# One group of small products a unit in batches 1 to 3 of a linear-attention and mixer kernel

## The chip, the cores and the metric

The kernel runs on one core of one Trainium2 chip. The metric is the device time of one execution in microseconds (us); a lower time is better. A difference of under about 0.3% (1.4 us here) can't be told from no change with this kernel.

Engines carry the names that the profile gives them: PE is the matrix engine (PEld its weight loads), DVE the vector engine, ACT the scalar engine, POOL the third elementwise engine, SP the engine that issues the transfers. Products are written to PSUM, from which ACT or DVE copy them to SBUF.

## The reference

Two blocks stand one behind the other. The first is a gated linear attention over 4 batches, 8 heads, 768 steps and 48 channels; the second a mixer on the 4 x 768 x 384 result.

```
f = sigmoid(f_logit)
for t in range(S):
    state = f[:, :, t, :, None] * state + einsum('bhd,bhe->bhde', k[:, :, t], v[:, :, t])
    y[:, :, t] = einsum('bhd,bhde->bhe', q[:, :, t], state)
x = y laid out as (batch, seq, heads * head_dim)
h = x^T @ U @ V                       # low rank, over the sequence
u = x + h^T
out = u + relu(u @ w_ch1) @ w_ch2
```

The einsum of the state is the outer product of a step's key with its value. Everything is in float32.

## The kernel before

**Units.** A unit is one pair of heads of one batch: 4 batches of 4 units, 16 in all, numbered `n` from 0. The sequence of a unit is cut into 12 chunks of 64 steps. Gates are turned into running products inside a chunk, so that queries and keys can be scaled by them (DVE, functions `gates`, `keep`, `keys`, `read` and `queries` of `prepare`). What is left for PE is five groups of small products for each unit (function `attend`):

- `kept` (L1002, tile `pt`): 12 transposes of the scaled keys; ACT copies the result to `kb` (L1006), and `spread` makes `whole` (L1012), the chunks' decays, on ACT.
- `states` (L1026, tile `ds`): 24 products of `kb` with v, each chunk's addition to the state; ACT copies `ds` to `added` (L1034).
- `scan` (L1051): DVE runs through `added` with the decays in `whole`; the states go to `st` by POOL (batches 1 and 2) or ACT (batch 3).
- `scores` (L975, tile `sc`): 24 products of keys and queries inside the chunks; DVE masks them into `A` (L988).
- `read` (L1069, tile `y`): 22 products of queries with the states `st`, followed on ACT by a copy of two columns, `seen` (L1076).
- `inner` (L1087, added onto `y`): 24 products of `A` with v; ACT copies `y` to `x` (L1093).

Each of these products is run as two passes (the trace shows 48 records for 24 products). They use parts of the array, 48 or 64 rows by 64 columns; the transposes use 64 rows by 128 columns.

**What fills PE between them.** While the attention of batch b runs, the mixer of batch b-1 supplies large products over the whole array: `pz` (L300), `po` (L355, batch 0's) and `pw` (L389, the other batches). `Fill` spreads them by cost over the pieces that `steps` yields: each piece, an empty one too, is preceded by its share of large products. `joined` puts several functions into one piece and yields empty pieces in place of the others, so that the shares stay.

**The order in a step.** Step n of `steps` issues one piece with `inner` of n-2, `scores` of n-1 and `kept` of n; later one with `read` of n-1, `states` and `scan` of n. Between them lie the fronts of unit n+1 (`gates`, `keep`, `keys`, and `read_back`, `queries`, the place of which depends on `behind`). So each unit has two groups of small products, with large products around each.

**PSUM.** Tiles with the tag `big` (two banks each) have three buffers: `pt`, `ds`, `sc` and `y` take them in turn, in the order in which they are allocated; the mixer's `pp`, `put` and `pu` use the same ones. `pz`, `po` and `pw` have two buffers of their own. `kb` and `whole` have a single buffer.

**Who orders what.** PE runs in the order of the code everywhere. DVE and ACT run in the order of the code up to the beginning of batch 2; behind that a scheduler orders them, with raised priority for the mask and the scan. SP is ordered by the scheduler from the end of batch 0. In batch 3 DVE also forms sums of the weights (`sum_of_w`, L929) at the pieces listed in `turns`.

Of the kernel before, what the change touches and what calls it, by code (L numbers as in the profile page):

```python
# [10 lines left out]
F32 = mybir.dt.float32  # L11
# [10 lines left out]
PAD = 64  # L22
# [542 lines left out]
def factored_path(ctx, tc, q, k, v, f_logit, moe_U, moe_V, moe_w_ch1, moe_w_ch2, out, ok):  # L565
# [5 lines left out]
    B, H, S, D = q.shape  # L571
    P = nc.NUM_PARTITIONS
# [4 lines left out]
    HP = H // 2  # L577
# [5 lines left out]
    NU = B * HP  # L583
# [17 lines left out]
    ps_big = ctx.enter_context(tc.tile_pool(name="ps_big", bufs=3, space=bass.MemoryType.PSUM))  # L601
# [23 lines left out]
    def packed(n, nm):  # L625

        i = 2 * n + (nm == "q")
        return w2.rearrange("p c d -> p (c d)")[:, i * 2 * NBL * D : (i + 1) * 2 * NBL * D]

    def load(n, *names):  # L630

        b, hp = divmod(n, HP)
        for nm in names:
            if nm == "v":
                v_tiles[n] = three.tile([P, NBL, 2, D], F32, name="v_nat")
            for par in range(2):
                head = src[nm][b, 2 * hp + par]
                if nm in "kq" and n < HP:
                    if par == 0:
                        nc.sync.dma_start(  # L640
                            out=packed(n, nm).rearrange("p (h t) -> p h t", h=2),
                            in_=src[nm][b, 2 * hp : 2 * hp + 2].rearrange("h (p c) d -> p h (c d)", p=P),
                        )
                    continue
                if nm == "v" and par:

                    for s in range(2):
                        nc.sync.dma_start(
                            out=v_tiles[n][(1 - s) * C : (2 - s) * C, :, par, :],
                            in_=head.rearrange("(c s p) d -> s p c d", s=2, p=C)[s],  # L650
                        )
                    continue
                if nm == "v" or n < TURNED:
                    dst = v_tiles[n] if nm == "v" else nat[n % 2][nm]
                    nc.sync.dma_start(out=dst[:, :, par, 0:D], in_=head.rearrange("(c p) d -> p c d", p=P))
                    continue
                head = head.rearrange("(c i) d -> i c d", i=NB)
                for part in range(2):
                    p0 = par * PAD + part * NB
                    n_ch = min(NB, D - part * NB)  # L660
                    nc.sync.dma_start(  # L661
                        out=raw[n % 2][nm][p0 : p0 + NB, :].rearrange("p (c d) -> p c d", d=NB)[:, :, 0:n_ch],
                        in_=head[:, :, part * NB : part * NB + n_ch],
                    )
# [248 lines left out]
    w_places, x_places, v_places, room = [], [], [], {}  # L913
# [43 lines left out]
    def attend(n):  # L957

        b, hp = divmod(n, HP)
        T = units[n]  # L960
        vt = v_tiles[n]
        rows = [slice(par * PAD, par * PAD + D) for par in range(2)]
        chunk = [slice(c * C, (c + 1) * C) for c in range(NCH)]

        part = [slice(s * C, (s + 1) * C) for s in range(2)]
# [48 lines left out]
        def halves_of(n):  # L1014
            return [slice(0, D // 2), slice(D // 2, D)] if n == HP - 1 else [slice(0, D)]

        def states():

            M = D if b else PAD
            ds = ps_big.tile([P, 2, 512], F32, name="ds", tag="big")  # L1020
            for c in range(NBL):
                for s in range(2):
                    for par in range(2):

                        i = (c + (s & par)) % NBL
                        nc.tensor.matmul(  # L1026
                            ds[par * PAD : par * PAD + M, s, c * D : (c + 1) * D],
                            lhsT=T["kb"][part[s ^ par], par, i, 0:M], rhs=vt[part[s ^ par], c, par, :],
                            start=True, stop=True,
                        )  # L1030

            for r in rows if b else [slice(0, P)]:
                for e in halves_of(n):
                    nc.scalar.copy(  # L1034
                        added[r, 1:].rearrange("p (e c s) -> p e c s", c=NBL, s=2)[:, e],
                        ds[r, :, 0 : NBL * D].rearrange("p s (c e) -> p e c s", e=D)[:, e],
                    )
# [40 lines left out]
        def inner():  # L1078
# [17 lines left out]
            )  # L1096
            del units[n], v_tiles[n]

        return [kept, states, scan, scores, read, inner, mask, spread]

    ahead, here = {}, {}

    def front(n, *names):

        if n >= NU:
            return []
        if n not in ahead:
            names_of = ("gates", "keep", "keys", "read_back", "queries", "gates_end", "unpack_k", "unpack_q")
            ahead[n] = dict(zip(names_of, prepare(n)))
        return [ahead[n].pop(nm) for nm in names if nm in ahead[n]]  # L1110

    def rear(n, *names):

        if not 0 <= n < NU:
            return []
        if n not in here:
            here[n] = dict(zip(("kept", "states", "scan", "scores", "read", "inner", "mask", "spread"), attend(n)))
        return [here[n].pop(nm) for nm in names if nm in here[n]]

    def joined(*groups):  # L1120

        groups = [g for g in groups if g]
        for _ in groups[1:]:
            yield lambda: None
        if groups:
            yield lambda: [f() for g in groups for f in g]

    def steps(first, last):

        def behind(n):  # L1130

            return HP + 3 <= n < NU - 1

        for n in range(first, last):
            if n < NU:
                yield from joined(rear(n - 2, "inner"), rear(n - 1, "scores"), rear(n, "kept"))
            else:
                for piece in rear(n - 2, "inner") + rear(n - 1, "scores"):
                    yield lambda: None
                    yield piece  # L1140
            if behind(n):
                yield from front(n, "read_back", "queries")
            if n + 1 < NU and n + 1 not in v_tiles:
                load(n + 1, "v")
            yield from front(n + 1, "gates", "keep", "keys")
            yield from joined(rear(n - 1, "read"), rear(n, "states", "scan"))
            if not behind(n + 1):
                yield from front(n + 1, "read_back", "queries")
            if n + 1 == last:
                yield from rear(n - 1, "inner")  # L1150
                if n + 2 < NU:
                    load(n + 2, "v")

    def attention(pieces, fill):

        for piece in pieces:
            fill()
            piece()
        fill.rest()

    def beside(pieces, calls):

        for i, piece in enumerate(pieces):
            yield piece
            while calls and calls[0][0] <= i:
                calls.pop(0)[1]()
        assert not calls
# [15 lines left out]
    with tc.manual_schedule(engines={nc.vector.engine, nc.scalar.engine}):  # L1183
# [111 lines left out]
        n = len(m.seconds) // (NBL // 2)  # L1295
        todo, after = m.seconds[:-n], m.seconds[-n:]

        attention(second, Fill(todo, 10 + 10 * HP - (len(start) + len(m.firsts) - 1 - EARLY)))
        n = 2 * HP + 2
# [3 lines left out]
        pieces, fill = steps(n - 1, 3 * HP + 1), Fill(m.main, 10 * HP - 3)  # L1303
# [3 lines left out]
    for b in range(2, B - 1):  # L1307
        if b > 2:
            pieces, fill = steps(b * HP + 1, (b + 1) * HP + 1), Fill(m.main, 10 * HP)
# [1 line left out]
        attention(pieces, fill)  # L1311
        m = start_mixer(b, after)

    turns = 5, 7, 8, 13, 14, 15, 16, 18, 19, 22, 27
    early_sums = len(W_SUMS) - len(turns)
    for i in range(early_sums):
        sum_of_w(i)
    pieces = beside(steps((B - 1) * HP + 1, NU + 1),
                    [(t, lambda i=i: sum_of_w(i)) for i, t in enumerate(turns, early_sums)])
    todo = m.first(0) + m.ready(0) + m.halved(0)  # L1320
    attention(pieces, Fill(todo[:-1], 33))

    mixers = [m, mixer(B - 1)]
    NP = NBL // 2
# [10 lines left out]
    todo = of(0, "sums_of_x") + of(0, "fewer")  # L1335
    todo[5:5] = of(1, "sums_of_x") + m.second(0)[-1:]
    for i in range(len(pairs)):
        ahead, behind = of(i + 1, "fewer"), of(i, "second")
# [356 lines left out]
```

## Time and profile before

| | |
|---|---|
| Median of 3 runs | 466.35 us (465.92 to 467.19) |
| Span of the profiled execution | 463.2 us, first to last instruction |
| Median less span | 3.15 us (the page gives no time of the profiled execution beside its span) |
| PE busy | 455.2 us, 98% of the span |
| DVE, ACT, POOL busy | 351.4, 170.4, 48.5 us |
| Granted PE clock | 0.999 |

Batch 0's attention fills the first 35 us or so, batches 1 to 3 run from there to 316 us beside the large products of the batch before, and from 316 us on only the mixer of batches 2 and 3 is left. A row of the timeline gives the start of a run of like instructions, how long it took from its start to its modelled end, and in brackets the idle time before it with its releaser. Since products are pipelined, a run's end lies behind the next one's start; what a run takes of PE is the distance from its start to the next one's start.

### The profile page before, as it was taken

To read this page: it belongs to the slowest core of one execution; us is meant where nothing else is said; L and a number is where in the kernel's file an instruction comes from. 1 tells how busy PE (TensorE), PEld (TensorE's weight loads), DVE (VectorE), ACT (ScalarE), POOL (GpSimd) and SP (SyncE) were. 2 spreads that over 40 slices of the span, in tenths; PEclk is the share of its full clock that TensorE was granted. 3 is DMA by queue.
4 is the path that set the end of the run, shared out by engine and by line. 5 is a ranking of instruction groups with operands and counts; after the bars stand their busy time and mean duration, and the time that the engine had idled before them with its cause. 6 is when DMAs were issued, how large, how long until landed. Compare 5 with 4: busy or idle time off the path is not lost.

```text
span 463.2 us, 13016 instructions
## 1 busy us (share of the span) xinstructions
PE 455.2 (98%) x5639; PEld 394.5 (85%) x5639; DVE 351.4 (76%) x585; ACT 170.4 (37%) x323; POOL 48.5 (10%) x56
## 2 busy tenths in 40 slices
PE   8999999999999999999999999999999999999997
PEld 5886888875666578999898888899989999999996
DVE  6778788979999677676765559977797887858652
ACT  6785776562333143323322323451412311212200
POOL 2002445634112001010000000000000000000000
PEclk9999999999999999999999999999999999999999
DMA  9959997577777604504633030100000000000001
GB/s 194 186 139 212 227 217 180 150 119 103 124 113 118 107 18 53 78 1 89 77 52 74 14 61 4 28 3 21 18 1 1 35 1 23 13 1 35 1 36 39
DMA packets 148583, 34.35 MB, mean 74 GB/s; under 512 B 136934, under 2 KB 146982, under 8 KB 148518
## 3 DMA queue, kind: packets, MB, share of 16 engines
q1 hardware_dynamic: 147718, 33.29, 37.1%
q8 instruction: 46, 0.75, 0.7%
q10 hardware_dynamic: 800, 0.15, 0.2%
q14 instruction: 19, 0.16, 0.1%
HBM read 28.70 MB, written 4.72 MB: 72 GB/s over the span
## 4 chain that ended last, share of the span: by engine, by line
PE 80%; DVE 11%; ACT 3%; DMA 2%; issue 2%; SPq 2%; DVEq 0%; ACTq 0%
PE pw L389 27%; PE pz L300 21%; PE pp L495 12%; PE po L355 5%; PE y L1069 2%; PE sc L975 2%; PE ds L1026 2%; PE y L1087 2%; PE pt L1002 1%; SPq L661 1%; DVE late L894 1%; PE pt L777 1%; DVE late L876 1%; PE pt L835 1%; DMA other<-in_f_logit_dram 1%
## 5 line engine op out<-in xcount | busy, mean ns | idle before, releaser
L300 PE MATMUL pz<-uT,w 128*128 128x256 f32 x492 | 111.5, 382 | 0.3
L300 PEld LDWEIGHTS pz<-uT,w 128*128 128x128 f32 x492 | 91.7, 190 | 12.9 <-ACT uT L289 0.6
L389 PE MATMUL pw<-zw,w_raw 128*128 128x192 f32 x216 | 38.0, 329 | 0.0
L389 PE MATMUL pw<-w,z_all 128*128 128x192 f32 x216 | 37.3, 327 | 0.0
L335 ACT ACTIVATE z_all<-pz 128x512 f32<-128x512 f32 x33 | 19.6, 598 | 45.1 <-PE pz L300 44.7
L389 PEld LDWEIGHTS pw<-w,z_all 128*128 128x128 f32 x216 | 35.3, 190 | 0.5
L389 PEld LDWEIGHTS pw<-zw,w_raw 128*128 128x128 f32 x216 | 35.1, 190 | 0.6 <-issue 0.3
L101 POOL TENSOR_TENSOR w<-w_y,w_r 128x384 int32<-128x384 int32 x24 | 31.5, 1311 | 37.0 <-DVE w_y L100 22.5
L876 DVE TENSOR_TENSOR_SCAN late<-fz,late 128x768 f32<-128x768 f32 x12 | 21.1, 1755 | 9.4 <-ACT fz L871 9.3
L488 ACT ACTIVATE other<-other 128x512 f32<-128x512 f32 x18 | 11.3, 630 | 40.3 <-DVE other L204 40.3
L355 PE MATMUL po<-w,zw 128*128 128x384 f32 x72 | 25.2, 495 | 0.0
L355 PE MATMUL po<-w,z_all 128*128 128x384 f32 x72 | 24.7, 493 | 0.0
L1057 POOL COPY st<-added 128x576 f32<-128x576 f32 x8 | 12.4, 1556 | 113.8 <-DVE added L1051 113.8
L988 DVE TENSOR_TENSOR A<-sc,causal 128x768 f32<-128x768 f32 x16 | 15.2, 953 | 8.5 <-PE sc L975 8.5
L355 PEld LDWEIGHTS po<-w,zw 128*128 128x128 f32 x72 | 13.2, 190 | 9.6 <-issue 0.8
L894 DVE TENSOR_TENSOR_SCAN late<-fz,other 128x768 f32<-128x768 f32 x12 | 21.0, 1750 | 0.2
L355 PEld LDWEIGHTS po<-w,z_all 128*128 128x128 f32 x72 | 13.3, 190 | 8.9 <-DVE o L204 0.6
L488 ACT ACTIVATE z_all<-z_all 128x512 f32<-128x512 f32 x12 | 7.6, 631 | 34.1 <-DVE z_all L204 34.1
L1034 ACT COPY added<-ds 48x576 f32<-48x576 f32 (+2 forms) x29 | 17.8, 619 | 4.5 <-PE ds L1026 4.1
L495 PE MATMUL pp<-v_nat,late 128*128 128x128 f32 x152 | 19.1, 275 | 0.0
L1069 PEld LDWEIGHTS y<-st,qT 48*64 48x64 f32 x704 | 13.6, 137 | 6.2 <-issue 4.5
L98 DVE TENSOR_SCALAR w_y<-w_y 128x384 f32<-128x384 f32 (+3 forms) x27 | 12.1, 449 | 8.8 <-ACT w_y L91 8.8
(233 smaller groups left out, 872.1 us busy)
## 6 DMA issues: line engine op xcount, KB each, us to landing
w_raw<-in_moe_w_ch_dram SPq DMA_DIRECT2D x18, 384.0 KB, 3.6
out_dram<-o SPq DMA_DIRECT2D x17, 192.0 KB, 1.9
v_nat<-in_v_dram SPq DMA_DIRECT2D x16, 144.0 KB, 3.8
v_nat<-in_v_dram SPq DMA_DIRECT2D x32, 72.0 KB, 3.5
zw<-in_moe_w_ch_dram SPq DMA_DIRECT2D x6, 384.0 KB, 5.1
out_dram<-o SPq DMA_DIRECT2D x14, 96.0 KB, 2.2
w<-in_k_dram SPq DMA_DIRECT2D x4, 288.0 KB, 4.1
w<-in_q_dram SPq DMA_DIRECT2D x4, 288.0 KB, 4.2
```

Source lines behind the costliest of these rows:

```text
L101: nc.gpsimd.tensor_tensor(dst.bitcast(I32), shaped(y.bitcast(I32)), shaped(r), ALU.add)
L300: nc.tensor.matmul(pm[:, i * 2 * P : (i + 1) * 2 * P], lhsT=w1[:, m, o : o + P], rhs=uT[a][:, m, :], start=(m == 0), stop=(m == NDC - 1))
L335: nc.scalar.activation(z[a, c][:, k : k + 2, :].rearrange("p i t -> p (i t)"), pm, AF.Relu)
L355: nc.tensor.matmul(pm, lhsT=z[a, i // NI][:, i % NI, s * P : (s + 1) * P], rhs=w2[:, i, :], start=(i == 0), stop=(i == NFC - 1))
L389: nc.tensor.matmul(W["pm"][:, n * HM : (n + 1) * HM], lhsT=lhs[:, i, :], rhs=rhs[:, i, :], start=(i == 0), stop=(i == NI - 1))
L488: nc.scalar.activation(dst, dst, AF.Relu, scale=float(SIGNS[n]))
L495: nc.tensor.matmul(pm[:, i, r * P : (r + 1) * P], lhsT=room["w"](wn)[:, r * P : (r + 1) * P], rhs=x_node(a, xn), start=((xn, wn) == of[0]) ...
L876: nc.vector.tensor_tensor_scan(backwards(X, S - 1, S), backwards(f, S, S), backwards(ends, S - 1, S), 0.0, ALU.mult, ALU.add,)
L894: nc.vector.tensor_tensor_scan(Y, f[:, 0:S], starts, 0.0, ALU.mult, ALU.add)
L988: nc.vector.tensor_tensor(T["A"], sc[:, :, 0 : NBL * C].rearrange("p h (c i) -> p h c i", i=C), causal.unsqueeze(1).unsqueeze(1).broadcast ...
L1034: nc.scalar.copy(added[r, 1:].rearrange("p (e c s) -> p e c s", c=NBL, s=2)[:, e], ds[r, :, 0 : NBL * D].rearrange("p s (c e) -> p e c s", ...
L1069: nc.tensor.matmul(o(c % 2, par, c // 2), lhsT=T["q"][rows[par], chunk[c]], rhs=T["st"][rows[par], c, :], start=(c <= 2), stop=False, skip ...
```

## The change

`steps` now yields one piece with small products for each unit: `read` of n-2, `states` and `scan` of n-1, `scores` of n-1, `kept` of n, `inner` of n-2, in this order. The number of pieces of a step stays 10. `read_back` and `queries` of unit n always stand behind that piece. In the last step of a batch `read` and `inner` of the unit n-1 come as pieces of their own, as do those of the last unit of all.

`room_of_states` allocates the tile `ds` ahead of `read`'s `y`, so that the three buffers are taken in the order `ds`, `y`, `sc`, and `pt` of the same piece gets the buffer of `ds`.

`states` makes the first head's products 64 columns of the keys wide (`PAD`) and leaves the second head's at 48 in batches 1 to 3. The rows 48 to 63 of `ds` are written then too, and one copy of 112 partitions goes to `added`, where two copies of 48 stood. In batch 0 nothing changes.

`turns` and a number of shares in batch 3 (33, now 38) are set anew.

Counted in the order of both programs, from the first `kept` of batch 1 to the last `inner`, the runs of small products with large ones on both sides go from 28 to 19. Those that end with something else than the transposes `pt` go from 16 to 15.

PE in batch 2, units 8 to 10, before: `y` and `ds` stand in one group, `y`, `sc` and `pt` in the next, `pz` and `pw` are large products.

```order
L1069 MATMUL y<-st,qT 64x48 x22
L1026 MATMUL ds<-v_nat,kb 48x48 x24
L300 MATMUL pz<-uT,w_89 128x256 x12
L1087 MATMUL y<-v_nat,A 64x48 x24
L975 MATMUL sc<-qT,kz_131 64x64 x24
L1002 MATMUL pt<-ident,kz_130 128x64 x12
L300 MATMUL pz<-uT,w_89 128x256 x18
```

The same place now, where the products of `ds` alternate between 64 and 48 columns of keys:

```order
L1074 MATMUL y<-st,qT 64x48 x22
L1031 MATMUL ds<-v_nat,kb 64x48
L1031 MATMUL ds<-v_nat,kb 48x48
...
L975 MATMUL sc<-qT,kz_131 64x64 x24
L1002 MATMUL pt<-ident,kz_130 128x64 x12
L1092 MATMUL y<-v_nat,A 64x48 x24
L300 MATMUL pz<-uT,w_89 128x256 x12
```

The large products between the two groups are gone from there (they stand in longer runs elsewhere), `sc` and `pt` directly follow `ds`, and the products with v (L1092, before L1087) follow the transposes.

ACT in batch 1, one unit, before:

```order
L1076 COPY seen<-y 128x2
L1034 COPY added<-ds 48x576 x2
L1093 COPY x<-y 128x2x6x48
L1006 COPY kb<-pt 128x768
L1012 COPY whole<-whole_136 128x576
```

And now, the same unit:

```order
L1081 COPY seen<-y 128x2
L1039 COPY added<-ds 112x576
L1006 COPY kb<-pt 128x768
L1012 COPY whole<-whole_136 128x576
L1098 COPY x<-y 128x2x6x48
```

One copy empties `ds`, and the copy of `y` to `x` moved behind the copies that belong to the transposes.

ACT at the first whole group of batch 1 (unit 4's states), before: L335 empties large products, L91 and L92 convert the mixer's weights.

```order
L335 ACTIVATE zw<-pz 128x512
L91 ACTIVATE w_y<-w_raw 128x384
L92 ACTIVATE w_r<-w_raw 128x384
L1034 COPY added<-ds 48x576 x2
L335 ACTIVATE zw<-pz 128x512
```

And now:

```order
L335 ACTIVATE zw<-pz 128x512
L91 ACTIVATE w_y<-w_raw 128x384
L92 ACTIVATE w_r<-w_raw 128x384
L1039 COPY added<-ds 112x576
L1006 COPY kb<-pt 128x768
L1012 COPY whole<-whole_136 128x576
```

The copy still stands behind a pair of conversions, but the copy of the transposes follows it without large products between.

The diff, cut to its core:

```
+        def room_of_states():
+            T["ds"] = ps_big.tile([P, 2, 512], F32, name="ds", tag="big")
+
         def states():
-            M = D if b else PAD
-            ds = ps_big.tile([P, 2, 512], F32, name="ds", tag="big")
+            M = [PAD, D if b else PAD]
+            if "ds" not in T:
+                room_of_states()
+            ds = T["ds"]
...
                         nc.tensor.matmul(
-                            ds[par * PAD : par * PAD + M, s, c * D : (c + 1) * D],
-                            lhsT=T["kb"][part[s ^ par], par, i, 0:M], rhs=vt[part[s ^ par], c, par, :],
+                            ds[par * PAD : par * PAD + M[par], s, c * D : (c + 1) * D],
+                            lhsT=T["kb"][part[s ^ par], par, i, 0 : M[par]], rhs=vt[part[s ^ par], c, par, :],
                             start=True, stop=True,
                         )
-            for r in rows if b else [slice(0, P)]:
+            for r in [slice(0, sum(M))]:
...
         for n in range(first, last):
-            if n < NU:
-                yield from joined(rear(n - 2, "inner"), rear(n - 1, "scores"), rear(n, "kept"))
-            else:
-                for piece in rear(n - 2, "inner") + rear(n - 1, "scores"):
-                    yield lambda: None
-                    yield piece
-            if behind(n):
-                yield from front(n, "read_back", "queries")
+            read = rear(n - 2, "read")
+            yield from joined(rear(n - 1, "room") + read if read else [], rear(n - 1, "states", "scan"),
+                              rear(n - 1, "scores"), rear(n, "kept") + rear(n - 2, "inner"))
+            yield from front(n, "read_back", "queries")
             if n + 1 < NU and n + 1 not in v_tiles:
                 load(n + 1, "v")
-            yield from front(n + 1, "gates", "keep", "keys")
-            yield from joined(rear(n - 1, "read"), rear(n, "states", "scan"))
-            if not behind(n + 1):
-                yield from front(n + 1, "read_back", "queries")
-            if n + 1 == last:
+            if n + 1 < last:
+                yield from front(n + 1, "gates", "keep", "keys")
+                yield lambda: None
+            elif n < NU:
+                yield from front(n + 1, "gates", "keep")
+                yield from rear(n - 1, "read")
+                yield from front(n + 1, "keys")
                 yield from rear(n - 1, "inner")
                 if n + 2 < NU:
                     load(n + 2, "v")
+            else:
+                for _ in range(4):
+                    yield lambda: None
+                yield from rear(n - 1, "read")
+                yield lambda: None
+                yield from rear(n - 1, "inner")
...
-    turns = 5, 7, 8, 13, 14, 15, 16, 18, 19, 22, 27
+    turns = 6, 8, 9, 14, 15, 16, 17, 18, 20, 25, 29
...
-    attention(pieces, Fill(todo[:-1], 33))
+    attention(pieces, Fill(todo[:-1], 38))
```

More of the change, by code (lines that the diff above doesn't have):

```diff
@@ L1097, in inner @@
             del units[n], v_tiles[n]
-        return [kept, states, scan, scores, read, inner, mask, spread]
+        return [kept, states, scan, scores, read, inner, mask, spread, room_of_states]
     ahead, here = {}, {}
@@ L1116, in rear @@
         if n not in here:
-            here[n] = dict(zip(("kept", "states", "scan", "scores", "read", "inner", "mask", "spread"), attend(n)))
+            here[n] = dict(zip(("kept", "states", "scan", "scores", "read", "inner", "mask", "spread", "room"), attend(n)))
         return [here[n].pop(nm) for nm in names if nm in here[n]]
@@ L1128, in steps @@
     def steps(first, last):
-        def behind(n):
-            return HP + 3 <= n < NU - 1
         for n in range(first, last):
-            if n < NU:
-                yield from joined(rear(n - 2, "inner"), rear(n - 1, "scores"), rear(n, "kept"))
-            else:
-                for piece in rear(n - 2, "inner") + rear(n - 1, "scores"):
-                    yield lambda: None
-                    yield piece
-            if behind(n):
-                yield from front(n, "read_back", "queries")
+            read = rear(n - 2, "read")
+            yield from joined(rear(n - 1, "room") + read if read else [], rear(n - 1, "states", "scan"),
+                              rear(n - 1, "scores"), rear(n, "kept") + rear(n - 2, "inner"))
+            yield from front(n, "read_back", "queries")
             if n + 1 < NU and n + 1 not in v_tiles:
                 load(n + 1, "v")
-            yield from front(n + 1, "gates", "keep", "keys")
-            yield from joined(rear(n - 1, "read"), rear(n, "states", "scan"))
-            if not behind(n + 1):
-                yield from front(n + 1, "read_back", "queries")
-            if n + 1 == last:
+            if n + 1 < last:
[5 more added lines that the diff above has]
+                yield from front(n + 1, "keys")
                 yield from rear(n - 1, "inner")
```

## The prediction

> **What bounds the kernel now.** I read the page first, then the stretches by time, then what PE waited for. The page's first line and three stretches from the end of batch 0 to the end of batch 3:
>
> ```profile
> PE 455.2 (98%) x5639; PEld 394.5 (85%) x5639; DVE 351.4 (76%) x585; ACT 170.4 (37%) x323; POOL 48.5 (10%) x56
> ```
>
> ```profile
> 95.00:145.00 50.00, 49.21 (x894) 32.90 (x886) 44.04 (x62) 19.51 (x39) 10.25 (x7) 1.00 0.79 119
> 166.00:274.00 108.00, 108.00 (x1334) 96.85 (x1332) 75.24 (x104) 34.10 (x62) 3.63 (x3) 1.00 0.33 53
> 274.00:316.00 42.00, 41.85 (x886) 36.94 (x884) 32.65 (x52) 18.66 (x31) 0.00 (x0) 1.00 0.08 16
> ```
>
> The columns are length, then busy time of PE, PEld, DVE, ACT and POOL, the clock, DMA. PE is idle for 0.79 us in the first stretch, for nothing in the second and for 0.15 us in the third. So PE's own time makes the span there, and the change is worth what it takes from the sequence of PE, or adds to it as waits. What PE waited for in these stretches:
>
> ```profile
> PE ds L1026 <- issue: 0.6, 1, 0.6
> PE pt L1002 <- DVE kz L805: 0.2, 1, 0.2
> ```
>
> Together these are 0.8 us, both in batch 1, where DVE is busy for 44 of 50 us.
>
> Then the timeline of PE through one unit of batch 2, first column the start:
>
> ```profile
> 171.06 0.93 PE L975 MATMUL sc<-qT,kz 48*64 48x64 f32 x48
> 171.92 0.58 PE L1002 MATMUL pt<-ident,kz 64*128 64x64 f32 x12
> 172.44 5.45 PE L300 MATMUL pz<-uT,w 128*128 128x256 f32 x24
> 177.81 0.84 PE L1069 MATMUL y<-st,qT 48*64 48x48 f32 x42
> 178.45 0.24 PE L1026 MATMUL ds<-v_nat,kb 64*48 64x48 f32 x2
> ...
> 179.19 5.45 PE L300 MATMUL pz<-uT,w 128*128 128x256 f32 x24
> 184.56 0.92 PE L1087 MATMUL y<-v_nat,A 64*64 64x48 f32 x48
> 185.30 0.89 PE L975 MATMUL sc<-qT,kz 48*64 48x64 f32 x48
> 186.12 0.59 PE L1002 MATMUL pt<-ident,kz 64*128 64x64 f32 x12
> 186.64 8.04 PE L300 MATMUL pz<-uT,w 128*128 128x256 f32 x36
> ```
>
> From start to start, the two groups of a unit take 1.38 us (177.81 to 179.19) and 2.08 us (184.56 to 186.64).
>
> **Term 1: nine fewer visits to the small products.** A visit costs beside its products. The same 24 passes of `pz` between two runs of whole-array transposes, and `inner` alone between large products:
>
> ```profile
> 55.90 5.35 PE L300 MATMUL pz<-uT,w 128*128 128x256 f32 x24
> 61.08 0.82 PE L777 MATMUL pt<-ident,late 128*128 128x128 f32 x6
> ```
>
> ```profile
> 251.88 0.91 PE L1087 MATMUL y<-v_nat,A 64*64 64x48 f32 x48
> 252.73 2.86 PE L300 MATMUL pz<-uT,w 128*128 128x256 f32 x12
> ```
>
> 24 passes take 5.18 us there and 5.37 us (172.44 to 177.81) between small groups: 0.19 us a visit. `sc` takes 0.86 us behind a large product and 0.82 us behind `inner`: 0.04 us. `inner` takes 0.85 us ahead of a large product and 0.74 us ahead of `sc`: 0.11 us, and for `ds` and `y` about 0.15 us; the transposes take 0.52 us and pay nothing like it that I can see. Visits go from 28 to 19, those that don't end with transposes from 16 to 15: 9 x 0.23 + 0.13 = **2.2 us less** (1.8 to 2.6).
>
> **Term 2: wider products in `states`.** Batch 0 already has them at 64 columns for both heads:
>
> ```profile
> 17.30 0.92 PE L1026 MATMUL ds<-v_nat,kb 64*64 64x48 f32 x48
> 18.15 1.61 PE L835 MATMUL pt<-later,late 128*128 128x130 f32 x12
> ```
>
> That is 0.85 us against 0.74 (178.45 to 179.19) at 48, both ahead of a large product: 0.11 us for both heads. Now half are wide. If passes simply add up it is 0.06 us, if the wide ones set the pace 0.11; nothing excludes zero. I take 0.08, nearer to the middle: 12 units, **1.0 us more** (0 to 1.3). [...]
>
> **Term 3: transposes ahead of the products with v.** Eight groups now go from transposes (64 rows by 128 columns of the array) to `inner`. No row shows this pair undisturbed. The nearest is the way in, from `sc` to the transposes: 0.82 us (185.30) against 0.75 us where `y` follows `sc`:
>
> ```profile
> 311.64 0.93 PE L975 MATMUL sc<-qT,kz 48*64 48x64 f32 x48
> 312.39 0.86 PE L1069 MATMUL y<-st,qT 48*64 48x48 f32 x44
> ```
>
> The first of these stands behind `inner`, the second behind a large product, which costs 0.04 more, so the way in is 0.11 us. For the way out the bounds are 0 and 0.11; since the transposes pay nothing ahead of large products, I take 0.03: **0.25 us more** (0 to 0.9). [...]
>
> **Term 4: the transposes now wait for the copy of `ds`.** `pt` takes the buffer of `ds`, and only `sc` lies between. How fast the copy is:
>
> ```profile
> 179.38 1.30 ACT L1034 COPY added<-ds 48x576 f32<-48x576 f32 x2 [0.46 <-PE ds L1026]
> L1034 ACT COPY added<-ds 128x576 f32<-128x576 f32 x3 | 1.9, 636 | 0.0
> ```
>
> ```profile
> 24.04 0.81 ACT kb L1006
> 24.89 0.92 PE ds L1026 x48
> ```
>
> ACT, idle and waiting, starts 0.93 us after `ds` does (178.45); a copy of 128 partitions takes 0.64 us, so I give one of 112 the same; the chain of waits (the second pair of rows) has PE start 0.04 us after an ACT copy it waits for. The transposes can begin 1.61 us after `ds`. Without the wait they would begin after `ds` and `sc`:
>
> ```profile
> 143.18 0.24 PE L1026 MATMUL ds<-v_nat,kb 64*48 64x48 f32 x2
> ...
> 143.79 0.90 PE L1087 MATMUL y<-v_nat,A 64*64 64x48 f32 x47
> ```
>
> `ds` ahead of another small product takes about 0.59 us, with `sc`'s 0.82 that is 1.41. The wait is 0.2 us in each of eight groups, **1.6 us more** (0 to 2.0). With two copies it would be 0.64 longer; the widening buys that.
>
> In the first of the eleven groups with a wait, unit 4's, the copy stands behind two conversions of weights on ACT:
>
> ```profile
> 83.24 0.54 ACT L91 ACTIVATE w_y<-w_raw 128x384 f32<-128x384 f32 x1
> 83.69 0.54 ACT L92 ACTIVATE w_r<-w_raw 128x384 int32<-128x384 uint32 x1
> 84.14 1.26 ACT L1034 COPY added<-ds 48x576 f32<-48x576 f32 x2
> ```
>
> Before them stands the emptying of the last large product:
>
> ```profile
> L335 ACT ACTIVATE z_all<-pz 128x512 f32<-128x512 f32 x33 | 19.6, 598 | 45.1 <-PE pz L300 44.7
> ```
>
> 0.6 + 0.9 + 0.64 is 2.1 us after the group's start, with what the handover costs 2.2; the transposes are due after 1.5: **0.7 us more**. It costs nothing today, since the transposes do not follow.
>
> **Term 5: DVE in batch 1.** From one unit's `keep` to the next DVE takes 12.13 us:
>
> ```profile
> 117.59 1.76 DVE L876 TENSOR_TENSOR_SCAN late<-fz,late 128x768 f32<-128x768 f32 x1 [0.90 <-ACT fz L871]
> 129.72 1.76 DVE L876 TENSOR_TENSOR_SCAN late<-fz,late 128x768 f32<-128x768 f32 x1 [0.90 <-ACT fz L871]
> ```
>
> ```profile
> 122.74 4.14 PE L355 MATMUL po<-w,z_all 128*128 128x384 f32 x12
> 126.71 2.10 PE L355 MATMUL po<-w,zw 128*128 128x384 f32 x6
> ```
>
> PE's step in batch 1 is 24 passes of `po`, 2 x 3.97 us, and a joined group: 0.64 + 0.59 + 0.82 + 0.52 + 0.85 + waits, 3.6 us: 11.6. In the new order DVE runs `scan`, the mask, `read_back`, `queries`, `gates`, `keep` and `keys` in a row from the copy of `ds` (2.2 us after a group's start) to the keys that the next group's transposes need (11.6 + 2.2 after it). One round of 12.1 us ends 14.3 us after it, or 0.5 us late, less what can run before the copy. I take 0.3 us for the groups of units 6 and 7, in place of the 0.2 of term 4: **0.6 us more** (0 to 2.5). The group behind them has 30 passes ahead of it and room. The 0.8 us of waits of today belong to the old order and go: **0.8 us less**. In batch 2 at least 60 passes of `pz`, 13 us, lie between two joined groups, and I cost the keys there at nothing. In batch 3 it is only 24 to 36 passes of `pz` or `pw`, 5 to 8 us; but DVE is busy for 32.65 us of 42, so it has 9 us to spare over three groups. I cost it at nothing too; if that cover is gone, the first rival below has a second place.
>
> ACT's second copy is gone (12 x 0.64 us) and worth nothing: ACT is busy for 37%.
>
> **The sum.** -2.2 + 1.0 + 0.25 + 1.6 + 0.7 + 0.6 - 0.8 = +1.15 us on a span of 463.2. From 316 us on the order is the old one, so I carry it to the end and to the median of 466.35, which lies 3.15 us above the span: **467.5 us**, 0.25% more. About 0.3%, 1.4 us, can be told from no change, so I forecast no change that can be measured, leaning to slower.
>
> **The rivals.**
>
> *DVE sets the period of batch 1 (slower).* The place is the `kz` product ahead of `pt` in the groups of units 6 and 7. It decides once the keys end more than 2.2 us after the group's start. If the weights' conversions push DVE's first round by 1.2 us, both groups wait that much more, 2 x 1.2 = 2.4 us: 469.9. For it: 44 us busy of 50 and the existing wait for `kz`. Against: today's wait is 0.2 us in all. Chance 0.20.
>
> *Every new switch and wide pass is paid in full (slower).* Term 2 at 0.11 and term 3 at 0.11 us a group: +0.35 + 0.65, 468.5. [...] Chance 0.13, as a row bears out only the way into the transposes.
>
> *The copy is hidden (faster).* If PE covers the waits of term 4 altogether (1.6 + 0.7) and the wide products cost 0.04 us a unit instead of 0.08, the sum falls by 2.8: 464.7. Chance 0.22. For it: batch 0 shows `pt` in unbroken runs; against: the copy's own rows.
>
> That the merge doesn't happen is excluded by the order of the program. Another 0.05 stays for something slower that I don't see, a late load of a unit, say.
>
> **How the numbers follow.** The forecast has 0.40. Faster by over 0.3% (below 464.95) is the third rival, 0.22; slower by over 0.3% (above 467.75) the two slower ones and the rest, 0.38; within it the forecast, 0.40. The range, 464.6 to 469.8, reaches from the third rival to the first.
>
> **What would show it.** Right: a repeated wait of about 0.2 us of `pt` (L1002) for ACT's `added`, 0.7 in the first group; five small groups in a row, 3.5 to 3.7 us each; `ds` some 0.08 us longer. Wrong: no idle time of PE ahead of `pt` (then the third rival), waits of `pt` for DVE `kz` over 1 us (the first), or a new wait of `y` for `st` or of `pz` for ACT, which now waits for the scan ahead of `whole`.

## The result and the profile after

The changed kernel takes 474.17 us (median of 4 runs, 473.61 to 474.76) against 466.52 for the kernel before on the same chip: a ratio of 1.0167, 95% interval 1.0149 to 1.0185. It is 7.65 us slower, well outside the range of the prediction. The profiled executions have spans of 473.0 and 463.2 us. In the runs of the changed kernel the time lies 1.76 us above the span; if that holds for the kernel before, its profiled execution took 465.0 us, about 1.5 us under its median. So of the 9.8 us between the profiles about 2 are scatter.

The first line of the changed kernel's page, then the three stretches of the prediction (length, then busy time of PE, PEld, DVE, ACT, POOL):

```profile
PE 455.3 (96%) x5639; PEld 396.9 (84%) x5639; DVE 348.6 (74%) x585; ACT 162.8 (34%) x311; POOL 45.1 (10%) x56
```

```profile
95.00:145.00 50.00, 47.49 (x765) 32.73 (x764) 44.27 (x56) 16.18 (x32) 10.80 (x8) 1.00 0.72 103
166.00:274.00 108.00, 105.73 (x1310) 95.21 (x1309) 70.47 (x97) 29.21 (x54) 5.50 (x4) 1.00 0.31 49
274.00:316.00 42.00, 39.94 (x838) 34.78 (x839) 33.21 (x48) 18.30 (x30) 0.00 (x0) 1.00 0.13 26
```

PE is as busy as before, 455.3 against 455.2 us. The whole loss is idle time of PE, and it is in each of the three stretches: 2.5, 2.3 and 2.1 us where there were 0.8, 0.0 and 0.15. What PE waited for (total, times, longest; idle times under 0.15 us are not in this list):

```profile
PE y L1092 <- issue: 3.9, 4, 1.6
PE pt L1002 <- DVE kz L805: 2.4, 2, 1.5
PE pw L389 <- issue: 1.5, 1, 1.5
...
PE pz L300 <- ACT uT L289: 0.8, 1, 0.8
...
PE po L355 <- ACT h L199: 0.6, 1, 0.6
...
PE put L288 <- ACT uT L289: 0.5, 1, 0.5
...
PE put L288 <- DVE o L204: 0.3, 1, 0.3
```

Three kinds. **First**, breaks that wait for nothing the profile shows ("issue"): three in batches 2 and 3 inside the products with v, one ahead of `pw` behind such a group, 3.8 us together, and one of 1.6 us in batch 0. **Second**, the transposes wait 2.4 us for DVE's keys in batch 1 (0.2 before). **Third**, 2.2 us of waits at the ends of batches 1 and 2, where the mixer changes batch (the four lines with `h`, `uT` and `o`); none of them was there before.

One break, in PE's timeline of the changed kernel:

```profile
241.32 0.68 PE L1092 MATMUL y<-v_nat,A 64*64 64x48 f32 x32
242.95 0.45 PE L1092 MATMUL y<-v_nat,A 64*64 64x48 f32 x16 [0.95 <-issue]
243.33 0.92 PE L389 MATMUL pw<-zw,w_raw 128*128 128x192 f32 x4
```

It falls inside one function's 48 passes, all of whose operands were there for the first 32. I counted PE's records in the trace (weight loads, products, and those of its queue) ahead of each break: 5313 at 193.44 us, 6593 at 242.95, 8386 at 307.12, 8898 at 318.25, 962 in batch 0. Divided by 256 each leaves 193 or 194. (Of the kernel before's two breaks with "issue", the one of 0.42 us in batch 0, at 36.82 us, leaves 193 as well; the one of 0.57 us ahead of `ds` in batch 1 leaves 26 and is of another kind.) The page has this row on DMA queues (packets, MB):

```profile
q8 instruction: 46, 0.75, 0.7%
```

PE has 11,392 records, 44.5 times 256, and the queue moved 46 packets of 16 KB: about one packet for 256 instructions. **Theory A**: PE's instructions arrive in blocks of 256, that is 128 passes (each a load and a product). 128 small passes run in about 2.2 us (48 of `sc` took 0.82). If a whole block lies in a run of small products, PE is through before the next block is there. A joined group has 44 + 48 + 48 + 12 + 48 = 200 passes; the groups before had 92 or 108, and one, at the end of batch 1, 140; none of them holds a whole block. Rival B: the breaks are waits for another engine that the profile misses. Theory C: DVE sets the pace of batch 1 (the prediction's first rival). Theory D: the waits at the ends come from the new order there.

Batch 0 has the same code in both kernels. PE's busy time there (12 to 50 us) in the kernel before, in the changed one, and in the eighth kernel below, whose batch 0 is that of the kernel before:

```profile
12.00:50.00 38.00, 36.72 (x884) 29.91 (x883) 27.61 (x55) 27.13 (x63) 4.48 (x6) 1.00 0.80 178
```

```profile
12.00:50.00 38.00, 34.83 (x876) 28.48 (x875) 26.32 (x52) 25.59 (x60) 4.49 (x6) 1.00 0.77 169
```

```profile
12.00:50.00 38.00, 35.25 (x876) 28.62 (x875) 26.31 (x52) 25.71 (x60) 4.48 (x6) 1.00 0.75 168
```

So the 1.9 us there are no effect of the change: of twelve profiles with this start, the one shown of the kernel before happens to be the best.

### The profile page after: what moved, and what is told of

Its sections match the earlier page's. It is cut to its first block, busy times and chain, and to the rows that moved or that the text cites. A ratio compares the mean times of both kernels' runs of the same rounds, so it can differ in the third digit from the quotient of the medians.

```text
span 473.0 us, 12999 instructions
## 1 busy us (share of the span) xinstructions
PE 455.3 (96%) x5639; PEld 396.9 (84%) x5639; DVE 348.6 (74%) x585; ACT 162.8 (34%) x311; POOL 45.1 (10%) x56
## 4 chain that ended last, share of the span: by engine, by line
PE 82%; DVE 8%; ACT 4%; issue 3%; DMA 1%; SPq 1%; POOL 0%; ACTq 0%; DVEq 0%; POOLq 0%
PE pw L389 26%; PE pz L300 22%; PE pp L495 12%; PE po L355 7%; PE y L1092 2%; PE y L1074 2%; PE ds L1031 2%; PE pt L1002 2%; PE sc L975 1%; PE pt L777 1%; PE pt L835 1%; DMA w<-in_q_dram 1%; ACT added L1039 1%; PE put L288 1%; DVE late L894 1%
## 5 line engine op out<-in xcount | busy, mean ns | idle before, releaser
L335 ACT ACTIVATE z_all<-pz 128x512 f32<-128x512 f32 x33 | 19.7, 598 | 46.5 <-PE pz L300 46.3
L101 POOL TENSOR_TENSOR w<-w_y,w_r 128x384 int32<-128x384 int32 x24 | 30.2, 1257 | 36.0 <-DVE w_y L100 22.4
L1056 DVE TENSOR_TENSOR_SCAN added<-added,whole 128x576 f32<-128x576 f32 x12 | 16.1, 1344 | 12.0 <-ACT added L1039 12.0
L1062 POOL COPY st<-added 128x576 f32<-128x576 f32 x8 | 10.3, 1292 | 129.9 <-DVE added L1056 129.9
L894 DVE TENSOR_TENSOR_SCAN late<-fz,other 128x768 f32<-128x768 f32 x12 | 22.1, 1843 | 0.1
L1092 PE MATMUL y<-v_nat,A 64*64 64x48 f32 x768 | 15.7, 221 | 3.9 <-issue 3.9
L871 ACT ACTIVATE fz<-late 128x756 f32<-128x756 f32 x10 | 8.3, 831 | 31.3 <-DVE late L754 31.3
```

Source lines behind the costliest of these rows:

```text
L101: nc.gpsimd.tensor_tensor(dst.bitcast(I32), shaped(y.bitcast(I32)), shaped(r), ALU.add)
L335: nc.scalar.activation(z[a, c][:, k : k + 2, :].rearrange("p i t -> p (i t)"), pm, AF.Relu)
L894: nc.vector.tensor_tensor_scan(Y, f[:, 0:S], starts, 0.0, ALU.mult, ALU.add)
L1056: nc.vector.tensor_tensor_scan(states[:, of], added[:, of], T["whole"].rearrange("p e c -> p (e c)")[:, of], 0.0, ALU.add, ALU.mult)
L1092: nc.tensor.matmul(o(s, par, c), lhsT=T["A"][part[s ^ par], par, c, :], rhs=vt[part[s ^ par], c, par, :], start=False, stop=True, skip_gro ...
```

## The experiments

Each time stands beside runs of the kernel before on the same chip (466.3 to 466.9).

**1. Every later instruction 116 places on.**

```
-        busy(3)
+        busy(1)
+        pads(31)     # 62 passes of 64x16
```

> The changed kernel with 31 tiny products (62 passes) at its start in place of two of the three idle ones, so that every later instruction of PE stands 116 places further on; nothing else changes. Theory A (PE runs dry at the border of a block of 256 instructions when the whole block lies in a group of small products): the breaks at 193.4, 243.0, 307.1 and 318.3 us, 3.8 us in all, go, one of about 1.0 us appears in the group at 213 us; 3.3 us less, about 470.9, and every break is again at the same place of a block. Rival B (those breaks are waits for another engine that the profile does not show): no change, 474.2, breaks in the same products as before.

482.6 us (ratio 1.0304, interval 1.0225 to 1.0383). The total is of no use: the clock granted to PE fell to 0.93 and 0.89 in two stretches, and batch 0 now had breaks of 6.6 us in all. The places are: in batches 1 to 3 the four breaks are gone, one stands in the group that was at 213 us, and one of 0.8 us in batch 1; their sum falls from 4.7 to 1.3 us (gaps between neighbouring starts, less the usual distance). All are again at places that leave 193 or 194.

**2. The same, 240 places on** (62 tiny products).

> The same with 62 tiny products, 240 places further on. Theory A: the borders now cut off a whole block in five or six of the joined groups, of which two break ahead of the transposes; 6.0 us of breaks in batches 1 to 3 instead of 4.5, so 1.5 us more, about 475.7 (up to 1 us more if the tiny products outlast the two idle ones that they replace). Rival B: no change, 474.2.

477.12 us (ratio 1.0210, 1.0140 to 1.0279). Again disturbed at the start (the first transposes start 4.1 us later, 9.38 instead of 5.32) and by the clock. Breaks in batches 1 to 3:

```profile
PE y L1092 <- issue: 1.4, 3, 0.6
```

Three groups instead of the five or six expected: where the border falls just ahead of or in the transposes there was none. All three sit at 193 or 194. The size was wrong, and so were two of the places; what sets those two apart is told behind kernel 11.

**3. Products with v ahead of the transposes.**

```
-  rear(n - 1, "scores"), rear(n, "kept") + rear(n - 2, "inner"))
+  rear(n - 1, "scores"), rear(n - 2, "inner") + rear(n, "kept"))
```

> The changed kernel with the products with v ahead of the transposes in each joined group. If the waits of the transposes for the copy (0.2 us in each of eight groups) and for DVE's keys (2.4 us in two groups) are what I take them for, 0.85 us of other work now stands ahead of them: 1.6 + 1.7 us less, and 0.9 less for groups that end with transposes; the breaks of theory A stay, since the group has the same length: about 470.0. If the transposes' waits cost nothing that can be gained so, 474.2.

473.15 us (1.0130, 1.0065 to 1.0194): 1.0 less than the changed kernel, not 4.2. The group itself did what was expected. In the changed kernel an undisturbed one:

```profile
213.19 0.84 PE L1074 MATMUL y<-st,qT 48*64 48x48 f32 x42
213.82 0.25 PE L1031 MATMUL ds<-v_nat,kb 64*64 64x48 f32 x2
...
214.46 0.24 PE L975 MATMUL sc<-qT,kz 48*64 48x64 f32 x2
...
215.52 0.59 PE L1002 MATMUL pt<-ident,kz 64*128 64x64 f32 x12
216.04 0.91 PE L1092 MATMUL y<-v_nat,A 64*64 64x48 f32 x48
216.88 1.35 PE L300 MATMUL pz<-uT,w 128*128 128x256 f32 x5
```

and here:

```profile
211.82 0.84 PE L1074 MATMUL y<-st,qT 48*64 48x48 f32 x42
...
214.68 0.59 PE L1002 MATMUL pt<-ident,kz 64*128 64x64 f32 x12
215.19 1.13 PE L300 MATMUL pz<-uT,w 128*128 128x256 f32 x4
```

3.69 us becomes 3.37. But the waits of the transposes in batch 1 fell only from 2.4 to 1.9: PE came earlier, the keys did not. (0.8 of the 1.9 are put down to ACT's copy of `y` to `x`, which ended 0.07 us after the keys.) The four breaks of batches 2 and 3 stayed, 4.7 us instead of 3.8.

**4. Keys of units 6 and 7 without their multiplication.**

```
-                nc.vector.tensor_tensor(t, t, T[of], ALU.mult)
+                if not (nm == "k" and HP + 2 <= n < HP + 4):
+                    nc.vector.tensor_tensor(t, t, T[of], ALU.mult)
```

> The changed kernel without the multiplication of the keys of units 6 and 7 by their decays (left out, one DVE instruction of 0.96 us each). Theory C (DVE sets the period in batch 1): the waits of the transposes for these keys, 1.46 and 0.96 us, fall by 0.96 and 0.96 or more, so 1.9 us less or a little more, 472.2. If DVE has room and the keys wait for something else, no change, 474.2.

471.48 us (1.0096, 1.0070 to 1.0123): 2.7 less. The wait that is left:

```profile
PE pt L1003 <- DVE kz L754: 0.5, 1, 0.5
```

2.4 to 0.5, the 1.9 expected: theory C holds. The rest of the gain isn't the keys'; the breaks are shorter here as well (3.1 us in batches 2 and 3 instead of 3.8).

**5. The shift without touching the start:** the first 29 large products of batch 1 cut in two.

```
+COLUMNS = iter(29 * [[slice(0, 128), slice(128, 256)]] + 999 * [[slice(0, 256)]])
...
+    for of in next(COLUMNS): nc.tensor.matmul(pm[:, i * 2 * P : (i + 1) * 2 * P][:, of], ...
```

> The changed kernel with the first 29 large products of batch 1 (256 columns) cut into two of 128, which moves every later instruction of PE 116 places on without touching the start of the kernel. Theory A: the breaks inside batches 1 to 3 fall from 4.7 us to 1.2 to 1.3 us (one in the group that stood at 213 us), as in the first of these kernels; 3.3 us less, plus what the cutting costs, 470.9 to 471.5. Rival B: 474.2 plus the cutting.

472.4 us (1.0123, 1.0063 to 1.0183), 1.8 less, 0.9 above the range expected; the span is 2.0 less, 471.0. The break is in the group it was expected in, and the four old ones are gone; one of 0.5 us is in batch 1:

```profile
216.58 0.66 PE L1092 MATMUL y<-v_nat,A 64*64 64x48 f32 x26
218.12 0.56 PE L1092 MATMUL y<-v_nat,A 64*64 64x48 f32 x22 [0.88 <-issue]
```

Nothing about data or other engines changed, so rival B falls here.

**6. The same cutting in the kernel before.**

> The same cutting in the kernel before: what it costs by itself. Theory A: no group of the kernel before holds a whole block of 256 instructions wherever the borders stand, so nothing is gained: 466.4 plus the cutting, 0 to 0.6 us. If places on the border mattered there too, up to 1 us either way.

467.15 us (1.0004, 0.9983 to 1.0025): no break at a border in batches 1 to 3. The one ahead of `ds` is there as before, 0.57 us, in the same product although that now stands 116 places further on. The cutting costs 0.4 us, which is within the noise.

**7. Ends of the batches as before.**

```
-                yield from front(n + 1, "gates", "keep")
-                yield from rear(n - 1, "read")
-                yield from front(n + 1, "keys")
+                yield from front(n + 1, "gates", "keep", "keys")
+                yield from joined(rear(n - 1, "read"), rear(n, "states", "scan"))
```

> The changed kernel with the end of each batch as before: the states of the next batch's first unit are issued with the last read, ahead of the mixer's change of batch. Theory D (the waits at the ends of batches, 0.57 for h, 0.52 for uT, 0.29 for o and 0.78 for uT, come from the order that the change gives the ends): these go, 2.2 us less, 472.0. If they come from the joined groups in between, they stay, 474.2.

473.08 us (1.0135, 1.0089 to 1.0182): 1.1 less, the span 2.1 less. The four waits, 2.2 us, are gone, and 0.9 us of others stands in their place:

```profile
PE pz L300 <- DVE o L204: 0.5, 1, 0.5
...
PE y L1092 <- ACT seen L1081: 0.3, 1, 0.3
...
PE pz L300 <- ACT uT L289: 0.2, 1, 0.2
```

So 1.3 us of the span are the order's, and theory D holds for most of the waits. The rest is again shorter breaks, 2.7 us instead of 3.8 in batches 2 and 3. Why `po` waits for the copy of `h` in the new order I have not settled; that the mixer's tiles get other PSUM buffers is a guess.

**8. The wide first head and the one copy alone, in the kernel before.**

```
-            M = D if b else PAD
+            M = [PAD, D if b else PAD]
...
-            for r in rows if b else [slice(0, P)]:
+            for r in [slice(0, sum(M))]:
```

> The kernel before with the wider first head and the one copy of the states alone. By my term 2 the 12 units cost 0.08 us each, 1.0 us more, 467.4; if the loads of 64 columns cost nothing, 466.4; the earlier end of the copy is worth nothing there, since nothing on the path waits for it.

467.46 us (1.0011, 0.9991 to 1.0031), 0.75 more, within the noise. The group of `y` and `ds`:

```profile
179.76 0.84 PE L1069 MATMUL y<-st,qT 48*64 48x48 f32 x42
180.40 0.25 PE L1026 MATMUL ds<-v_nat,kb 64*64 64x48 f32 x2
...
181.22 3.07 PE L300 MATMUL pz<-uT,w 128*128 128x256 f32 x13
```

1.46 us instead of 1.38: 0.08 a unit, term 2 as predicted; the other such groups of batches 1 to 3 grow by 0.08 or 0.09 as well.

**9. Edits 3 and 7, batch 1's large products moved, and five groups cut.** Besides the edits shown:

```
-  rear(n - 1, "scores"), rear(n - 2, "inner") + rear(n, "kept"))
+  rear(n - 1, "scores"), *([] if n in (10, 12, 14, 15, 16) else [rear(n - 2, "inner") + rear(n, "kept")]))
+  yield from joined(rear(n - 2, "inner") + rear(n, "kept"))
...
-  Fill(todo, 10 + 10 * HP - ...
+  Fill(todo, 7 + 10 * HP - ...
```

> Four edits of the changed kernel together: products with v ahead of the transposes, batch ends as before, batch 1's large products spread over three pieces fewer (30 passes instead of 24 ahead of the groups of units 7 and 8, so that DVE has more time), and the five groups in which a whole block of instructions lay cut in two behind the scores by a share of large products. If the theories A, C and D and the reading of the inner-first run are right: 2.0 + 1.7 + 1.1 to 1.9 + 4.4 less, 5 x 0.23 = 1.2 more for the cuts: 465.4 to 466.2, about the kernel before. If the breaks were waits for something else, the cuts only add: 470 or more.

472.0 us (1.0129, 1.0094 to 1.0163): a miss. With 30 passes ahead of the groups, 6 fewer were left at the end of the batch, and a wait came there:

```profile
PE y L1092 <- issue: 2.7, 3, 1.3
PE y L1092 <- ACT seen L1081: 2.1, 2, 1.9
```

Two of the cuts, in batch 3, did nothing: no large product was due at that piece.

**10. The five cuts alone**, in the changed kernel.

> The changed kernel with one edit: those five joined groups are cut in two behind the scores, with a share of large products between the scores and the transposes. Theory A: their breaks go without any shift of the later instructions, 4.3 us less, 1.2 more for five visits, and up to 5 x 0.2 = 1.0 less where the large products cover the wait for the copy: 470.1 to 471.1. Rival B (hidden waits for another engine ahead of the products with v): these products come later by a share of large products and the wait may be covered as well, but then the break behind the group at 318 us, ahead of pw, stays: 471.5 or more.

473.31 us (1.0139, 1.0112 to 1.0166), 0.9 less. That is 2.2 us above the range of theory A, and by the time alone rival B would have it. The places decide. The two groups of batch 2 that were cut have no break any more; the two of batch 3 in which nothing came between kept theirs, in the products with v and ahead of `pw` (one of the two `y` below is in batch 0):

```profile
PE pw L389 <- issue: 1.6, 1, 1.6
PE y L1092 <- issue: 1.5, 2, 1.0
```

So a cut helps where large products stand in it. The fifth group, the first whole one of batch 3, had no break to lose.

**11. The disputed cost by itself:** in the kernel before, the scores of one unit eight times over.

```
-            for c in range(NBL):
+            for c in (8 if n == 9 else 1) * list(range(NBL)):
```

> The kernel before with the score products of one unit of batch 2 issued eight times over into the same place: one run of 384 passes, 768 instructions, that depends on nothing new and that nothing new waits for. At 0.0171 us a pass (0.82 us for 48) it lasts 6.6 us. Theory A: three borders of blocks of 256 instructions lie in it, and at the last two PE has run through a whole block in 2.2 us, less than a block needs to arrive; two breaks of 1.2 to 1.7 us at these borders, 256 instructions apart, and the run lasts 9.0 to 10.0 us: 466.4 + 5.75 + 2.4 to 3.4 = 474.6 to 475.6. Rival B (breaks are hidden waits for other engines): no break, since there is nothing to wait for; 472.2.

476.51 us (1.0222, 1.0199 to 1.0245). PE's timeline:

```profile
186.75 2.56 PE L975 MATMUL sc<-qT,kz 48*64 48x64 f32 x161
190.30 2.09 PE L975 MATMUL sc<-qT,kz 48*64 48x64 f32 x128 [0.98 <-issue]
194.30 1.62 PE L975 MATMUL sc<-qT,kz 48*64 48x64 f32 x95 [1.91 <-issue]
195.86 0.59 PE L1002 MATMUL pt<-ident,kz 64*128 64x64 f32 x12
```

Two breaks, exactly 128 passes apart, in products that wait for nothing. The run lasts 9.1 us instead of 6.6. From break to break 4.00 us pass for 128 passes that run in 2.1. (The profiled run took 474.6 us, within the range expected, and the median lies 0.9 above it.) Theory A is shown.

The packets of the instruction queue say more exactly what PE waits for. Paired off in order, one packet goes with each block. All kernels together have 32 breaks in batches 1 to 3 at 193 or 194. At each of them the block's packet started 0.6 to 1.6 us after PE had begun the block ahead of it, and PE went on 1.2 to 1.6 us after the packet's end. A whole block inside a group is not enough for a break, though. Two joined groups of the changed kernel hold one and run through, this one of batch 1 and the one at 293.91 us:

```profile
135.38 0.84 PE L1074 MATMUL y<-st,qT 48*64 48x48 f32 x42
...
138.22 0.92 PE L1092 MATMUL y<-v_nat,A 64*64 64x48 f32 x48
139.07 1.24 PE L355 MATMUL po<-w,z_all 128*128 128x384 f32 x3
```

Their packets had started 2.7 and 2.1 us before the block ahead began. In the two groups of kernel 2 without the expected break they had started 0.2 and 0.6 us before it. The same holds for all 20 blocks in batches 1 to 3 of these kernels that PE left within 3.2 us without a break: the packet of the next one had started before they began. So a break in these batches needs a whole block among small products and a packet that starts late; what makes the queue start some packets earlier stays open.

**12. What helped, together:** edits 3 and 7, 31 cut products, and one group cut (`n in (11,)`).

> The edits that helped, together: products with v ahead of the transposes (2.0 less), batch ends as before (1.7 less), 31 large products of batch 1 cut (124 places on: breaks from 4.4 to 1.0, plus 0.45 for the cutting) and the one joined group that then still holds a whole block cut behind the scores (1.0 less, 0.23 more). 474.2 - 2.0 - 1.7 - 3.0 - 0.8 = 466.7, the kernel before within 0.3%; the waits for DVE's keys in batch 1, 1.9 us, stay. If the gains don't add up, 468 to 470.

471.15 us (1.0096, 1.0075 to 1.0117): 3.0 less than the changed kernel, still 4.6 above the kernel before, and a miss by either of the two numbers expected. Batches 2 and 3 have no break at a border left, but `pz` now waits 1.4 us for DVE there. In batch 1 two breaks came:

```profile
112.21 0.79 PE L1092 MATMUL y<-v_nat,A 64*64 64x48 f32 x36 [1.09 <-issue]
...
126.14 0.33 PE L1092 MATMUL y<-v_nat,A 64*64 64x48 f32 x6 [1.87 <-issue]
```

DVE's keys there:

```profile
111.28 0.96 DVE L805 TENSOR_TENSOR kz<-kz,late 128x768 f32<-128x768 f32 x1
...
123.78 0.96 DVE L805 TENSOR_TENSOR kz<-kz,late 128x768 f32<-128x768 f32 x1
```

They end at 112.24 and 124.74, so the first break in part takes the place of the wait for the keys: the transposes behind it start 0.7 us after them. Those behind the second start 1.7 us after them. The gains don't add up. More data is moved in batch 1 (a mean busy share of the DMA engines of 0.71 against 0.36 between 180 and 250 us of the changed kernel), but that blocks come later for it isn't shown: these two packets took 0.99 and 1.53 us, those of the changed kernel's four breaks 0.88 to 1.40. No version here beats the kernel before.

## Why the prediction was wrong

**What bounds the kernel** was read rightly: PE's sequence. The step that failed is the sentence "the change is worth what it takes from the sequence of PE, or adds to it as waits", in which I counted waits for other engines alone. PE also waits for its own instructions, and the sum had no term for it. That is 3.8 us of the loss in the profile, for which the kernel before had nothing in batches 1 to 3, since none of its groups there holds a whole block.

**Terms 1 to 4** came out nearly as sized, and cancel. A unit's two groups took 1.38 + 2.08 = 3.46 us, the joined one takes 3.69 with the waiting transposes, 3.37 without; with 0.19 us for the way in saved, the joining gains 0.28 a unit (0.23 less 0.08 had been forecast, so 0.15), and the wait with the switch costs 0.32 (0.23 forecast). Together they are nearly nothing, as PE's busy time says. The forecast wait itself is in the rows: from `sc` to the transposes 1.06 us pass (214.46 to 215.52) instead of 0.82. Term 2 is confirmed by kernel 8 (0.08 us a unit). The 0.7 us in unit 4's group were wrong: that group has no `y`, so `pt` takes the third buffer and waits for nothing (transposes at 93.65 us, copy from 93.62 on). The first groups of batches 2 and 3 are built alike and take the same 2.07 us.

**Term 5** had the mechanism and a quarter of the size: 0.6 us forecast, 2.4 measured. The step was "I take 0.3 us for the groups of units 6 and 7". Keys in the changed kernel and before:

```profile
110.54 0.96 DVE L805 TENSOR_TENSOR kz<-kz,late 128x768 f32<-128x768 f32 x1
...
123.04 0.96 DVE L805 TENSOR_TENSOR kz<-kz,late 128x768 f32<-128x768 f32 x1
```

```profile
108.74 0.96 DVE L805 TENSOR_TENSOR kz<-kz,late 128x768 f32<-128x768 f32 x1
...
120.86 0.96 DVE L805 TENSOR_TENSOR kz<-kz,late 128x768 f32<-128x768 f32 x1
```

DVE's round is 12.5 us now, 12.1 before, and PE's step 11.6 by term 5's estimate (in kernel 4 it is 12.0 from group to group, 107.50 to 119.50, 0.46 of them a wait). Where DVE's round is the longer one, what PE saves comes back as a wait. I had put this down as a rival (2.4 us more, chance 0.20), and its sign came, a wait of 1.46 us; its row says what I should have given it: DVE busy for 44 of 50 us.

**The ends of batches** were costed at nothing without being looked at: the diff moves `states` of a batch's first unit over the mixer's change of batch, and 2.2 us of waits appeared there; kernel 7 takes them away and puts 0.9 in their place.

For the profile: 3.8 + 2.2 (keys, 2.4 less 0.2) + 2.2 + 1.9 (batch 0, scatter) - 0.6 (the old break ahead of `ds`) = 9.5 of the 9.8 us between the spans. Without batch 0 it is 7.6, beside 7.65 between the medians; that these agree so closely is in part luck, since the breaks at the same places came to 3.1 us in kernel 4 and 4.7 in kernel 3.

## What to carry to other kernels

By these runs, a group of small products is worth joining only while no block of 256 instructions lies in it whole, or where the borders are known and shifted (1.8 us less in kernel 5; groups of up to 140 passes had no break at a border in batches 1 to 3 of any of these kernels): a break "issue" inside a run of like products, at the same remainder of the instruction count (193 or 194 here), is the sign. Where the engine beside the bound had a round longer than the bound's (DVE's 12.1 us, PE's step 11.6 by my estimate), work taken from the bound turned into waits for it (2.4 us). And the gains measured one at a time, several of them in the same group, didn't add up: 3.0 us less in kernel 12 where 7.5 were expected.

## What the runs showed of the hardware

- 32 breaks of PE in batches 1 to 3 stand where the count of its instructions, divided by 256, leaves 193 or 194 (the one ahead of `ds` in the kernel before leaves 26). Two of them, in kernel 11, are 128 passes apart in products that wait for nothing. The queue moved 46 packets of 16 KB for 11,392 records of PE in the changed kernel, about one for 256. At the 32 borders with a break in batches 1 to 3, 2.9 to 4.1 us passed from the border before, and PE stood still for 0.3 to 1.9 of them; from border to border it is, for example, 3.3 (190.16 to 193.44), 3.7 (239.28 to 242.95) or 4.0 (kernel 11). For the break at 193.44 the queue's packet starts at 190.78, 0.6 us after the block's first instruction, and takes 1.38; PE goes on 1.28 after it. A border cost no idle time where the packet had started before the block ahead began: 2.7 and 2.1 us before it in two joined groups of the changed kernel, which ran through a whole block in 1.84 and 1.82 us.
- Where PE starts with tiny products instead of two of the three idle ones, the clock granted to it was lower for a while: in kernel 1 it was 0.93 between 12 and 35 us, 0.89 between 50 and 95 and 0.97 between 95 and 145, in kernel 2 only 0.97 between 95 and 145. Why was not tried, and the start need not be the cause: two of the thirteen runs of the kernel before on the same chip had a mean clock of 0.984 too, at 471.3 and 471.4 us.
